# A recurrent mixer with two gated layers: each pair's inputs in three transfers, first key-value products earlier, first output sums later

## Chip, cores, metric

The kernel runs on one core of a Trainium2 chip. The metric is device microseconds of one execution, the median of several runs. Beside them there is one execution taken by the hardware profiler; every time of the trace below is counted in microseconds from the first instruction of that execution.

## What is computed

The reference, cut to what matters (batch 4, 8 heads, 768 steps, head size 48; 3072 tokens of width 384; hidden sizes 1536 and 2048):

```python
state = zeros(B, H, D, D)
for t in range(768):
    cur = einsum('bhd,bhe->bhde', u * k[t], v[t])
    y[t] = einsum('bhd,bhde->bhe', r[t], state + cur)
    state = w[t][..., None] * state + einsum('bhd,bhe->bhde', k[t], v[t])
x = y as (3072, 384)
x = (sigmoid(x @ w_gate) * (x @ w_val)) @ moe_w_out
h = x @ moe2_w_in
out = (h * tanh(softplus(h))) @ moe2_w_out
```

## The kernel before

**Tiling.** The 768 steps are cut into 24 steps j of 32 time steps; two of them are a pair p = 0..11. A pair gives 256 rows of the first gated layer, so the first layer runs as twelve rounds, one for each pair; two rounds give 512 rows of the second layer. Products are made of a high and a low half of type f16, so each weight exists twice (w_gate as wgs, w_val as wvs, moe_w_out as wos, moe2_w_in as wis, moe2_w_out as wps); the weights are decoded on the chip from 64-bit words (raw_wg, raw_wv, raw_wo, raw_wi, raw_wp) by ACT, DVE and POOL.

**A pair's own work ("attention").** `load_pair` (line 414) brings r, k and w of a pair into one tile blk, double buffered by the pair's parity: 1280 KB, of which r is 384, k 512 and w 384 KB. `fine` (457) makes on POOL products of r and k (tiles pt; 128x768 with u, then 128x384) and lets DVE sum them into A; between its three levels POOL multiplies r, k and w by w (blk<-blk). r and k are needed from the first product on, w from the first multiplication by w. `coarse` (548) flips r, k, w on DVE (RD, KD, WD), makes lp on PE, flips A into X and merges lp into it (line 618). `keys` (639) finishes k and flips it into KT, the last read of blk. `step` (664) makes for each j the output rows yp (`rows_out`, from X, v, RD and the state s), splits them into two halves xs (`split`, line 200) and brings them to xt, for the first two pairs by flips on PE (xp, line 699), later by a transposing DMA; it makes the next state from the key-value products kp (`outer`, 778, with the bank of PSUM that `next_at` names, three in turn) and loads v of step j+3.

**Rounds.** `gate(p, f)` (814) makes for one f of 12 the gate and value sums gv (18 matmuls, four banks pg in turn, three in round 0) and from them gt, on ACT and DVE. `out1(p, c, part)` (880) sums a quarter of the output o of column block c, in one bank, po; after the fourth quarter ACT and DVE split it into xo, and SP stores xo to x2d. Round p holds the gates of pair p, the output sums of pair p-1 and the attention of pair p+1. From 634 us on there is only the second layer: h (line 1013) and its output sums (1058).

**Order.** Nothing runs in the order of the code. `Plan.run` (87) plays all tasks with written costs, gives each a latest due time, and at each moment takes on each engine the ready task that is due first; the order that comes out is each engine's program. Who must wait for whom on the chip is then set by the tiles: a DMA into blk waits for the last reader of the pair two before. All DMAs of the page stand in the one queue of SP in the planned order, except the transposing ones, which ACT issues; an issue that waits holds all behind it. Every engine runs its own list in order.

The part of `load_pair` that sets how many transfers a pair has:

```python
if p:
    attn("sp", 3.6, lambda e: go(e, None), [], keys, lat=2.0)
else:
    attn("none", 0, new, [], keys, lat=0.0)
    for i in range(3):
        attn("sp", 1.2, lambda e, i=i: go(e, i), [], [keys[i]], lat=2.0)
```

Of the kernel before, what the change touches and what calls it, by code (L numbers as in the profile page):

```python
# [24 lines left out]
DM = H * D  # L25
# [126 lines left out]
def mixer_moe_kernel(  # L152
# [245 lines left out]
    kd = {}  # L398
    wd = {}
    lps = {}  # L400
    yps = {}
    kps = {}
    xss = {}
# [10 lines left out]
    def load_pair(p):  # L414
        edges = (0, C * DH, C * (DH + DP), BLK)

        def new(e):
            blk[p] = fp.tile([128, BLK], F32, tag=f"blk{p % 2}", name=f"blk{p}")

        def go(e, i):  # L420
            if i is None:
                new(e)
            cs = slice(0, BLK) if i is None else slice(edges[i], edges[i + 1])
            nc.sync.dma_start(out=blk[p][:, cs], in_=rkw[p, :, cs])

        keys = [("blk", p % 2, i) for i in range(3)]
        if p:
            attn("sp", 3.6, lambda e: go(e, None), [], keys, lat=2.0)
        else:
            attn("none", 0, new, [], keys, lat=0.0)  # L430
            for i in range(3):
                attn("sp", 1.2, lambda e, i=i: go(e, i), [], [keys[i]], lat=2.0)

    def load_v(j):
        def go(e):
# [228 lines left out]
    def step(j):  # L664
        p, e = divmod(j, 2)
        V = ("v", j % 3)
        S, nxt = ([("s", i % 2, x) for x in range(2)] for i in (j, j + 1))
        ybank = next_at()

        def rows_out(part):  # L670
            if not part:
# [43 lines left out]
                    out=xt[p][:, i, :, 128 * e : 128 * e + 128], in_=xss[j][:, i]  # L715
                )

        for part in range(2):
            attn(
                "pe",  # L720
                0.8 * (COLD if j < 4 else 1.0),
                lambda _, part=part: rows_out(part),
                [("X", p % 2), ("RD", p % 2), V, *S],
                [ybank],
                burst=True,
            )
        xs = ("xs", j % 2)
        split(
            xs,
            lambda: yps[j][:, :DM],  # L730
            lambda: xss[j][:, 0],
            lambda: xss[j][:, 1],
            SX,
            0.45,
            [ybank, "attention"],
            new_xs,
        )
        reads = [(*xs, 0), (*xs, 1)]
        room = [("xt", p % 2, 0, 0)] * e
        if p < 2:  # L740

            tbank = next_at()
            attn("pe", 0.6, flip_x, [*reads, "eye"], [tbank])
            attn("act", 0.48, lambda on: put(on, 0), [tbank, *room], [("xt", p % 2, e, 0)])
            room = [("xt", p % 2, 0, 0)]
            attn("dve", 0.48, lambda on: put(on, 1), [tbank, *room], [("xt", p % 2, e, 1)])
        else:
            new = [("xt", p % 2, e, i) for i in range(2)]
            attn("act", 0.15, send, [*reads, *room], new, lat=2.8)
        if j + 1 == NJ:  # L750
            return

# [14 lines left out]
        for hf in range(2):  # L767
            if j:
                attn(
                    {"pool": 1.05, "dve": 0.6},  # L770
                    0,
                    lambda on, hf=hf: decay(on, hf),
                    [S[hf], ("WD", p % 2)],
                    [nxt[hf]],
                )
            kbank = next_at()

            def outer(_, hf=hf, kbank=kbank):
                kps[j, hf] = pp.tile([128, 8, D], F32, tag=f"at{kbank[1]}", name=f"kp{j}_{hf}")
                for i in range(8):  # L780
                    x = 8 * hf + i
                    for o in (0, 32, 64, 96):
                        nc.tensor.matmul(  # L783
                            kps[j, hf][o : o + 32, i, :],
                            KT[o : o + 32, p % 2, HG * e + x, :],
                            vs[j][o : o + 32, x, :],
                            start=True,
                            stop=True,
                        )

            def join(_, hf=hf):
                s = ss[j + 1][:, 8 * hf : 8 * hf + 8]
                if j:
                    nc.vector.tensor_tensor(out=s, in0=kps[j, hf], in1=s, op=ALU.add)
                else:
                    nc.vector.tensor_copy(out=s, in_=kps[j, hf])

            cold = COLD if j < 4 else 1.0
            attn("pe", 0.8 * cold, outer, [("KT", p % 2), V], [kbank], burst=True)
            attn("dve", 0.55, join, [kbank], [nxt[hf]])  # L800
        if j + 3 < NJ:
            load_v(j + 3)

# [376 lines left out]
    for p in range(NP):  # L1180
        for f in range(NF1):
            if p + 1 < NP:
                if f == YPOS[0]:
                    tail1(p + 1)
                if f == YPOS[1]:
                    tail2(p + 1)
                    if p + 2 < NP:
                        cells[p + 2] = fine(p + 2)
                    else:
                        tail_end()  # L1190
            if f == 0 and p >= NP - 1:
                load_x2(0)
                load_x2(1)
            gate(p, f)
            if p > 0:
                out1(p - 1, f // 4, f % 4)
    add("none", 0, lambda e: None, [], ["gates", "free_g"])
    add(
        "act",
# [61 lines left out]
```

## Time and profile before

| | us |
|---|---|
| median of 3 runs (lowest to highest) | 1024.71 (1020.68 to 1025.45) |
| the profiled execution, its own time | 1025.36 |
| its span, first to last instruction | 1023.6 |
| PE busy in the span | 941.2 (92%) |
| DVE, ACT, POOL busy | 512.9, 347.1, 307.6 |
| mean granted clock of PE, of full speed | 0.988 |

The profile's page gives busy time by engine and, in 40 slices of 25.6 us, how busy each engine and the 16 DMA engines were. PE is idle for 82.4 us of the span, all of it in the first 634 us. A wait is put down to what ended it; "issue" stands for an idle time that ended with nothing that the profile shows. PEq, SPq and ACTq are the sequencers that hand instructions to an engine or a queue. The queue kind "instruction" in the DMA views carries programs to the engines.

### The profile page before, as it was taken

Reading aid. Unit: us, or ns where it says so; the run is one execution under the profiler, and the core shown is the slowest. Engines: PE = TensorE matmul, PEld = TensorE weight load, DVE = VectorE, ACT = ScalarE, POOL = GpSimd, SP = SyncE. Lnnn points to the kernel's source line nnn. Section 1 sums busy time; section 2 is a strip of 40 time slices with the busy share of each in tenths; the row PEclk is TensorE's granted clock in tenths of the full one; section 3 lists DMA queues with packets and bytes.
Section 4 is the critical chain, followed back from the end, with each engine's and each line's share of the span. In section 5 each row is a group of like instructions: output and inputs, shape, how many; then the busy total and the mean of one; then the engine's idle time right before and its main releaser. Section 6 shows DMA issues by size and latency. Waiting matters only on the chain.

```text
span 1023.6 us, 32777 instructions
## 1 busy us (share of the span) xinstructions
PE 941.2 (92%) x14952; PEld 678.8 (66%) x14952; DVE 512.9 (50%) x831; ACT 347.1 (34%) x693; POOL 307.6 (30%) x322
## 2 busy tenths in 40 slices
PE   0388789989999899989999999999999999999998
PEld 0266678868878687878888887655555555555555
DVE  5899988866666556666658557221111111111110
ACT  3347622212212122222226356433333333333320
POOL 8873589671744444454113011000000000000000
PEclk9999899989999899999999999999999999999999
DMA  9345543222140404040206351010100101000000
GB/s 303 125 168 177 198 95 110 45 100 91 33 91 29 90 28 90 29 100 20 60 9 173 107 175 42 11 37 16 41 14 16 39 16 47 9 16 16 8 16 31
DMA packets 53595, 72.12 MB, mean 70 GB/s; under 512 B 20432, under 2 KB 37328, under 8 KB 52048
## 3 DMA queue, kind: packets, MB, share of 16 engines
q1 hardware_dynamic: 36816, 66.09, 21.2%
q10 hardware_dynamic: 16640, 3.94, 2.4%
q8 instruction: 117, 1.92, 0.8%
q14 instruction: 22, 0.18, 0.1%
HBM read 56.64 MB, written 9.44 MB: 65 GB/s over the span
## 4 chain that ended last, share of the span: by engine, by line
PE 78%; DVE 9%; DMA 4%; issue 3%; POOL 2%; ACT 2%; ACTq 0%; SPq 0%; DVEq 0%
PE gv L828 22%; PE o L1058 18%; PE h L1013 18%; PE o L892 11%; PE yp L680 3%; PE kp L783 3%; PE lp L595 3%; DMA raw_wo<-wo 1%; POOL pt L455 1%; DVE A L476 1%; POOL blk L455 1%; DVE word_wi L286 1%; DMA raw_wp<-wo 1%; DMA raw_wv<-wv 1%; DVE X L611 1%
## 5 line engine op out<-in xcount | busy, mean ns | idle before, releaser
L1013 PE MATMUL h<-x,wis 128*128 128x512 f16 x864 | 201.5, 379 | 0.0
L828 PE MATMUL gv<-xt,wgs 128*128 128x256 f16 x1296 | 167.4, 277 | 11.7 <-DVE gt L859 5.7
L828 PE MATMUL gv<-xt,wvs 128*128 128x256 f16 x1296 | 168.1, 276 | 4.3 <-issue 4.3
L892 PE MATMUL o<-gt,wos 128*128 128x256 f16 x1296 | 167.5, 275 | 4.4 <-DVE xo L207 1.9
L455 POOL TENSOR_TENSOR blk<-blk 128x384 f32<-128x384 f32 (+1 forms) x144 | 125.9, 890 | 70.0 <-DVE KD L566 59.3
L828 PEld LDWEIGHTS <-wgs 128*128 128x128 f16 x1296 | 124.9, 99 | 30.5 <-issue 12.6
L1013 PEld LDWEIGHTS <-wis 128*128 128x128 f16 x864 | 84.5, 98 | 90.7
L892 PEld LDWEIGHTS <-wos 128*128 128x128 f16 x1296 | 127.2, 98 | 24.2 <-issue 4.8
L828 PEld LDWEIGHTS <-wvs 128*128 128x128 f16 x1296 | 121.9, 99 | 23.4 <-issue 4.6
L839 ACT ACTIVATE sig<-gv 128x256 f32<-128x256 f32 x144 | 55.0, 383 | 236.4 <-PE gv L828 225.2
L1024 ACT ACTIVATE e<-h 128x512 f32<-128x512 f32 x96 | 57.3, 597 | 207.5 <-PE h L1013 207.5
L455 POOL TENSOR_TENSOR pt<-blk 128x384 f32<-128x384 f32 (+1 forms) x96 | 108.4, 1154 | 51.4 <-DMA blk<-rkw 47.3
L844 DVE SCALAR_TENSOR_TENSOR gv<-gv,sig 128x256 f32<-128x256 f32 x144 | 61.7, 429 | 82.7 <-ACT sig L839 82.2
L856 ACT CAST gt<-gv 128x256 f16<-128x256 f32 x144 | 53.2, 371 | 76.1 <-DVE gv L844 69.1
L859 DVE TENSOR_TENSOR gt<-gv,gt 128x256 f16<-128x256 f32 x144 | 60.3, 419 | 32.2 <-ACT gt L856 32.1
L595 PE MATMUL lp<-RD,KD 64*16 64x16 f32 (+1 forms) x3072 | 34.5, 185 | 37.0 <-DVE RD L560 33.6
L1031 DVE SCALAR_TENSOR_TENSOR wos<-e,wos 128x512 f16<-128x512 f32 x27 | 18.7, 692 | 84.5 <-ACT wos L1027 84.5
L595 PEld LDWEIGHTS lp<-RD,KD 64*16 64x16 f32 (+1 forms) x3072 | 29.8, 101 | 46.1 <-DVE RD L560 33.6
L1058 PE MATMUL o<-wps,wgs 128*128 128x384 f16 x324 | 58.5, 326 | 0.0
L1058 PE MATMUL o<-wps,wos 128*128 128x384 f16 x324 | 57.2, 326 | 0.0
L1031 DVE SCALAR_TENSOR_TENSOR wgs<-e,wgs 128x512 f16<-128x512 f32 x27 | 18.7, 692 | 73.8 <-ACT wgs L1027 73.8
L783 PE MATMUL kp<-v,KT 32*32 32x48 f32 x2944 | 45.9, 212 | 8.6 <-issue 7.5
(92 smaller groups left out, 1051.0 us busy)
## 6 DMA issues: line engine op xcount, KB each, us to landing
blk<-rkw SPq DMA_DIRECT2D x11, 1280.0 KB, 6.7
v<-vt SPq DMA_DIRECT2D x96, 96.0 KB, 3.3
raw_wi<-wi SPq DMA_DIRECT2D x8, 768.0 KB, 4.9
raw_wp<-wo SPq DMA_DIRECT2D x8, 768.0 KB, 4.4
raw_wg<-wg SPq DMA_DIRECT2D x6, 768.0 KB, 4.5
raw_wv<-wv SPq DMA_DIRECT2D x6, 768.0 KB, 4.8
raw_wo<-wo SPq DMA_DIRECT2D x6, 768.0 KB, 4.4
x2d<-xo SPq DMA_DIRECT2D x36, 128.0 KB, 1.8
```

The costliest lines, as they stand in the source:

```text
L455: engines[e].tensor_tensor(out=pv, in0=a, in1=b, op=ALU.mult)
L595: nc.tensor.matmul(out, kd[p][gs, x, :m], rhs, start=True, stop=True, skip_group_check=True)
L783: nc.tensor.matmul(kps[j, hf][o : o + 32, i, :], KT[o : o + 32, p % 2, HG * e + x, :], vs[j][o : o + 32, x, :], start=True, stop=True,)
L828: nc.tensor.matmul(gps[p, f][:, o], w[:, a, kc, fs], xt[p][:, c, kc, :], start=(n == 0), stop=(n == 3 * KC - 1),)
L839: nc.scalar.activation(out=sgs[p, f], in_=gps[p, f][:, 0], func=AF.Sigmoid, scale=1.0 / (SW * SX))
L844: nc.vector.scalar_tensor_tensor(out=gps[p, f][:, 1], in0=gps[p, f][:, 1], scalar=SG / (SW * SX), in1=sgs.pop((p, f)), op0=ALU.mult, op1=A ...
L856: nc.scalar.copy(out=gt[p][:, 0, f], in_=gps[p, f][:, 1])
L859: nc.vector.tensor_tensor(out=gt[p][:, 1, f], in0=gps[p, f][:, 1], in1=gt[p][:, 0, f], op=ALU.subtract,)
L892: nc.tensor.matmul(ops[p, c][:, :NT], wos[:, a, f, cs], gt[p][:, g, f, :], start=(f == 0 and n == 0), stop=(f == NF1 - 1 and n == 2),)
L1013: nc.tensor.matmul(hps[r, f], w2["wi"][:, a, kc, fs], x2[r][:, c, kc, :], start=(n == 0), stop=(n == 3 * KC - 1),)
L1024: nc.scalar.activation(out=es[r, f], in_=hps[r, f], func=AF.Mish, scale=ih)
L1058: nc.tensor.matmul(ops2[r, t][:, :DM], g2[r][f][:, c, tsl], w2["wp"][:, a, f, :], start=(f == 0 and n == 0), stop=(f == NF2 - 1 and n == 2),)
```

## The change

Three edits, all in the task list that the plan works on.

1. Pairs 0, 2 and 3 are loaded in three transfers (r, k, w) that are queued one after the other. Pairs 4 to 11 have them apart: r is listed where the whole load was (round p-3, gate 7), k after gate 11 of round p-3 and after the last store of out1 of that round, w after gate 3 of round p-2 and after the first store of that round. Pair 1 keeps one transfer.
2. In step 0 the key-value products and the state made of them are listed ahead of the outputs, and take their banks first.
3. The twelve quarters of out1 of pair 0 are listed two at a time behind gates 6 to 11 of round 1, not one behind each gate.

```diff
+    late = {}
@@ load_pair
-        if p:
+        if p == 1:
             attn("sp", 3.6, lambda e: go(e, None), [], keys, lat=2.0)
-        else:
-            attn("none", 0, new, [], keys, lat=0.0)
-            for i in range(3):
-                attn("sp", 1.2, lambda e, i=i: go(e, i), [], [keys[i]], lat=2.0)
+            return
+
+        after = [[], [("x2d", p - 4, KC - 1)], [("x2d", p - 3, 0)]]
+        attn("none", 0, new, [], keys, lat=0.0)
+        for i in range(3):
+            late[p, i] = lambda i=i: attn(
+                "sp", 1.2, lambda e: go(e, i), after[i] if p > 3 else [], [keys[i]], lat=2.0
+            )
+            if p <= 3 or i == 0:
+                late.pop((p, i))()
@@ step
-        ybank = next_at()
+        ybank = tbank = None
...
+        def outputs():
+            nonlocal ybank, tbank
+            ybank = next_at()
...
+        if j:
+            outputs()
         if j + 1 == NJ:
             return
...
             attn("dve", 0.55, join, [kbank], [nxt[hf]])
+        if not j:
+            outputs()
@@ the loop over rounds p and gates f
             gate(p, f)
-            if p > 0:
+            if p > 1:
                 out1(p - 1, f // 4, f % 4)
+            elif p == 1 and f >= 6:
+                for n in (2 * f - 12, 2 * f - 11):
+                    out1(0, n // 4, n % 4)
+            if f == 3 and p > 1 and (p + 2, 2) in late:
+                late.pop((p + 2, 2))()
+            if f == 11 and (p + 3, 1) in late:
+                late.pop((p + 3, 1))()
```

The body of `outputs` is what stood in `step` before, moved in by one level.

**The queue of SP around the turn from round 5 to round 6** (blk7 to blk10 are pairs, v a step's values, x2d<-xo a store of the first layer's output). Before:

```order
L928 DMA x2d_86<-xo_5408 128x512
L424 DMA blk9_5815<-rkw 128x2560
L440 DMA v15_5915<-vt 32x768 x4
L928 DMA x2d_86<-xo_5788 128x512
L440 DMA v16_6118<-vt 32x768 x4
L928 DMA x2d_86<-xo_6148 128x512
```

Changed:

```order
L945 DMA x2d_86<-xo_5753 128x512
L447 DMA v15_5834<-vt 32x768 x4
L447 DMA v16_6082<-vt 32x768 x4
L425 DMA blk9_6099<-rkw 128x768
L945 DMA x2d_86<-xo_6112 128x512
L425 DMA blk8_5214<-rkw 128x1024
L945 DMA x2d_86<-xo_6245 128x512
L425 DMA blk8_5214<-rkw 128x768
```

The whole load of pair 9 ahead of v15 has become r of pair 9 behind v16; k and w of pair 8 stand behind the stores of o14_2 and o15_0, a round later than its whole load stood before.

**DVE at the same turn** (gv6_0 is the first gate of round 6, pt the product with u that POOL makes of r and k, A its sums, xo<-o15_0 what the second of those stores sends). Before:

```order
L455 TENSOR_TENSOR pt_5943<-pt_5943,U_93 128x768
L844 SCALAR_TENSOR_TENSOR gv5_11_6059<-gv5_11_6059,sig_6135 128x256
L207 SCALAR_TENSOR_TENSOR xo_6148<-o14_2_5866,xo_6148 128x256
L476 TENSOR_REDUCE A_91<-pt_5943 128x32
L859 TENSOR_TENSOR gt5_5321<-gv5_11_6059,gt5_5321 128x256
```

Changed:

```order
L876 TENSOR_TENSOR gt6_6153<-gv6_1_6117,gt6_6153 128x256
L462 TENSOR_TENSOR pt_6198<-pt_6198,U_93 128x768
L861 SCALAR_TENSOR_TENSOR gv6_2_6178<-gv6_2_6178,sig_6222 128x256
L483 TENSOR_REDUCE A_91<-pt_6198 128x32
L207 SCALAR_TENSOR_TENSOR xo_6245<-o15_0_6139,xo_6245 128x256
```

The product with u, which waits for POOL and so for k, has moved from the end of round 5 to behind gate 1 of round 6, three instructions ahead of the split of o15_0.

**PE at the start, from the first lp on** (kp0_0 and kp0_1 are the two halves of the first key-value products; the flips xp0 follow in both). Before:

```order
L595 MATMUL lp0_242<-RD0_232,KD0_229 32x24 x64
L595 MATMUL lp0_242<-RD0_232,KD0_229 16x16 x64
L680 MATMUL yp0_398<-v0_114,X0_226 32x48 x16
L783 MATMUL kp0_0_419<-v0_114,KT_92 32x48 x32
L680 MATMUL yp0_398<-v0_114,X0_226 32x48 x16
L699 LDWEIGHTS xs0_484
```

Changed:

```order
L602 MATMUL lp0_242<-RD0_232,KD0_229 32x24 x64
L602 MATMUL lp0_242<-RD0_232,KD0_229 16x16 x64
L798 MATMUL kp0_0_395<-v0_114,KT_92 32x48 x32
L798 MATMUL kp0_1_434<-v0_114,KT_92 32x48 x32
L688 MATMUL yp0_475<-v0_114,X0_226 32x48 x16
L688 MATMUL yp1_497<-v1_124,X0_226 32x48 x4
```

Both halves of kp0 stand ahead of yp0; kp0_1 stood behind the six flips xp0 before, and yp1, which needs the state made of both, behind that.

**DVE at the end of round 0's gates** (word_wo is the decoding of moe_w_out). Before:

```order
L286 SCALAR_TENSOR_TENSOR word_wo4_1734<-raw_wo4_1569,word_wo4_1734 128x768
L275 SCALAR_TENSOR_TENSOR word_wo5_1783<-word_wo5_1783,low_wo5_1771 128x768
L300 TENSOR_TENSOR wos_90<-word_wo4_1734,wos_90 128x768
L286 SCALAR_TENSOR_TENSOR word_wo5_1783<-raw_wo5_1707,word_wo5_1783 128x768
L859 TENSOR_TENSOR gt0_807<-gv0_11_1686,gt0_807 128x256
```

Changed:

```order
L876 TENSOR_TENSOR gt0_778<-gv0_11_1579,gt0_778 128x256
L612 TENSOR_TENSOR KD2_1208<-KD2_1208,WD2_1600 128x32x8
L612 TENSOR_TENSOR RD2_1424<-RD2_1424,WD2_1600 128x32x8
L275 SCALAR_TENSOR_TENSOR word_wo0_1468<-word_wo0_1468,low_wo0_1526 128x768
L618 STREAM_TRANSPOSE X2_1830<-A_91 128x32x32
```

All decoding of moe_w_out, which stood ahead of the last gate of round 0, now begins behind it.

## Rows read from the trace of the kernel before

**Rows 1.** The page's span, busy times and PE's line of its 40 slices.

```profile
span 1023.6 us, 32777 instructions
PE 941.2 (92%) x14952; PEld 678.8 (66%) x14952; DVE 512.9 (50%) x831; ACT 347.1 (34%) x693; POOL 307.6 (30%) x322
...
PE   0388789989999899989999999999999999999998
...
```

**Rows 2.** PE's waits from 190 to 460 us: total, times, longest.

```profile
PE gv L828 <- issue: 8.6, 2, 4.3
PE yp L680 <- issue: 3.8, 2, 2.7
PE o L892 <- issue: 1.8, 1, 1.8
PE kp L783 <- issue: 0.8, 2, 0.4
```

**Rows 3.** The same view from 460 to 634 us, where no pair is loaded.

```profile
PE gv L828 <- DVE gt L859: 1.3, 1, 1.3
PE o L892 <- DVE xo L207: 1.0, 3, 0.5
```

**Rows 4.** Stretches: length, PE, PEld, DVE, ACT, POOL busy (instructions), PEclk, DMA share, GB/s.

```profile
160.00:170.00 10.00, 10.00 (x94) 8.96 (x92) 9.25 (x15) 3.92 (x9) 9.84 (x9) 1.00 0.42 144
...
200.00:210.00 10.00, 5.66 (x163) 4.47 (x162) 4.78 (x7) 1.52 (x4) 0.42 (x1) 0.94 0.93 228
208.80:215.60 6.80, 5.83 (x85) 4.18 (x86) 1.37 (x4) 0.76 (x2) 5.87 (x6) 0.50 0.24 63
352.10:358.90 6.80, 5.59 (x84) 3.94 (x84) 0.95 (x1) 0.00 (x0) 4.20 (x5) 0.50 0.11 19
...
500.00:510.00 10.00, 10.00 (x206) 8.65 (x204) 6.61 (x12) 2.18 (x6) 0.83 (x1) 1.00 0.28 75
```

**Rows 5.** DMA queues from 341.5 to 350.5 us: packets, MB, share.

```profile
q1 hardware_dynamic: 298, 1.64, 80.6%
q10 hardware_dynamic: 832, 0.20, 20.3%
```

**Rows 6.** The same view from 500 to 512 us, the program's own queue.

```profile
q8 instruction: 2, 0.03, 1.2%
```

**Rows 7.** PE in order of time: start, length, instructions, [idle before, what ended it].

```profile
47.31 0.36 PE L783 MATMUL kp<-v,KT 32*32 32x48 f32 x2 [3.73 <-issue]
...
411.84 2.13 PE L828 MATMUL gv<-xt,wgs 128*128 128x256 f16 x18
...
421.67 1.15 PE L892 MATMUL o<-gt,wos 128*128 128x256 f16 x9
...
425.39 0.82 PE L892 MATMUL o<-gt,wos 128*128 128x256 f16 x6
```

**Rows 8.** SP's issues around the turn from one round to the next.

```profile
393.67 0.33 SPq L424 DMA_DIRECT2D blk<-rkw  x1
...
412.91 0.34 SPq L928 DMA_DIRECT2D x2d<-xo  x1
```

**Rows 9.** POOL after that load.

```profile
399.88 2.75 POOL L455 TENSOR_TENSOR pt<-blk 128x768 f32<-128x768 f32 x2 [5.99 <-DMA blk<-rkw]
402.71 1.98 POOL L455 TENSOR_TENSOR blk<-blk 128x384 f32<-128x384 f32 x2
```

**Rows 10.** The loads of blk: a piece of pair 0 (count, KB, us to landing); all loads.

```profile
blk<-rkw SPq DMA_DIRECT2D x2, 384.0 KB, 4.1
...
DMA to landing us min/median/max: 3.2/6.3/10.5
```

**Rows 11.** PE's waits from 61 to 180 us.

```profile
PE gv L828 <- DVE gt L859: 4.5, 3, 2.4
...
PE lp L595 <- POOL KD L605: 2.0, 1, 2.0
```

**Rows 12.** Decoding moe_w_out on DVE: count, ns min/median/max, first and last start.

```profile
L275 DVE SCALAR_TENSOR_TENSOR word_wo<-word_wo,low_wo x6: 926/951/1379, 95.5 to 119.6; 128x768 uint32<-128x768 uint32 x6
```

More of the change, by code (lines that the diff above doesn't have):

```diff
@@ L716, in send @@
                 )
[L718 to L725, printed above, removed]
-            )
[L727 to L749, printed above, removed]
+        def outputs():
+            nonlocal ybank, tbank
+            ybank = next_at()
+            for part in range(2):
+                attn(
+                    "pe",
+                    0.8 * (COLD if j < 4 else 1.0),
+                    lambda _, part=part: rows_out(part),
+                    [("X", p % 2), ("RD", p % 2), V, *S],
+                    [ybank],
+                    burst=True,
+                )
+            xs = ("xs", j % 2)
+            split(
+                xs,
+                lambda: yps[j][:, :DM],
+                lambda: xss[j][:, 0],
+                lambda: xss[j][:, 1],
+                SX,
+                0.45,
+                [ybank, "attention"],
+                new_xs,
+            )
+            reads = [(*xs, 0), (*xs, 1)]
+            room = [("xt", p % 2, 0, 0)] * e
+            if p < 2:
+                tbank = next_at()
+                attn("pe", 0.6, flip_x, [*reads, "eye"], [tbank])
+                attn("act", 0.48, lambda on: put(on, 0), [tbank, *room], [("xt", p % 2, e, 0)])
+                room = [("xt", p % 2, 0, 0)]
+                attn("dve", 0.48, lambda on: put(on, 1), [tbank, *room], [("xt", p % 2, e, 1)])
+            else:
+                new = [("xt", p % 2, e, i) for i in range(2)]
+                attn("act", 0.15, send, [*reads, *room], new, lat=2.8)
```

## The prediction

> **What bounds the kernel now.** I read the page first, to see which engine has no room: PE is busy for 941 of 1023.6 us and full from the 25th slice on, so whatever is gained must come out of the first 634 us, where its slices hold 7s and 8s [rows 1]. I then asked for PE's waits by stretch, since an average over the start, the rounds and the second layer says nothing on any of them. From 190 to 460 us PE waited in seven places, 15.0 us together, and every one ended with "issue": it waited for no engine [rows 2]. From 460 to 634 us, with the same rounds but no pair left to load, not one such wait is listed and 2.3 us are lost in all [rows 3]. So the difference between the two stretches is the thing to explain.
>
> What is special about the seven places shows in the stretches and the queues. From 200 to 210 us the 16 DMA engines were 0.93 busy while PE was busy for 5.66 of 10 us; from 500 to 510, with loads of v and transposing DMAs but no pair, 0.28 and 10.00 [rows 4]. In the 9 us around the load of 340.9 us only the two data queues moved packets; of the queue that carries PE's program there is none, while in 12 undisturbed us it moves two [rows 5, 6]. My reading: PE runs out of program because the blocks of its program arrive behind 1280 KB of a pair. One row supports that from the other side: at 160 to 170 us a pair is loaded too (DMA 0.42) and PE does not stop, because there it issues only 94 matmuls in 10 us, against 163 in the 5.7 busy us of the stretch at 200 [rows 4]. A load hurts where yp and kp run, with hundreds of short matmuls, and not where gates run.
>
> The longest two waits cost more than their length: at 208.8 to 215.6 and 352.1 to 358.9 us the granted clock was 0.50, the lower level of 1.2 GHz, just after PE had stood idle for over 4 us [rows 2, 4]. PE was busy there for 5.83 and 5.59 us, half of which, 5.7 us, is lost. The load of pairs therefore costs 15.0 + 5.7 = 20.7 us now.
>
> The Trainium skill says otherwise of the mechanism: Runtime: NRT & Kernel Launch, Instruction fetch mechanics, has the program streamed in 16 KiB blocks ahead of need, with the cost of crossing a block "mostly hidden". By that page the seven waits would not be the load's doing, and the sum would be the start-up term alone; the rows at 200 and 341.5 us speak against it, and it stands below as a rival.
>
> **Edit 1, three transfers apart.** It removes nine loads of 1280 KB and adds 27 smaller ones. On SP that is 18 issues more of 0.33 us each, on a queue that waits most of the time: nothing on PE's path. What matters is where the pieces fall. Let T0 be the first gate of a round, 411.84 in the example [rows 7]. The last store of the round before was issued at T0 + 1.1 [rows 8]; r now stands ahead of it, behind v, and k right behind it, so k is issued at about T0 + 1.5. That is the stretch of pure gates in which a load did no harm. w stands behind the store of the first output sum, whose last quarter ends at T0 + 10.8; the split and the store bring w to about T0 + 12.7, alone, with 384 KB. The dense matmuls at the end of a round keep only v and the transposing DMAs, as from 460 us on. So nearly the whole 20.7 should go. What I hold back is the turn into round 2 and round 2 itself, where k and w of pair 4 share the queue with raw_wi3 and raw_wi4, 768 KB each: 3.2 us. I take **17.5 us**; ends 12 and 20.7.
>
> Edit 1 also adds waits. Behind k: POOL's product for u, and behind that DVE's product with u, after which gate 2, a sum and the split of the first output block stand on DVE. The next output sum on PE needs that split, since there is one bank, and it begins at T0 + 13.5 [rows 7]. Counting back four operations of DVE (split, sum, gate, product) at no more than the 0.95 us of a 128x768 one [rows 12] and one of POOL at 1.4 (half of the first of [rows 9]), k must have landed by about T0 + 8.3. How long it takes is not in the trace: a piece of 384 KB took 4.1 us, the whole pair from issue to POOL's start 6.2 us [rows 8 to 10], which gives T0 + 5.6 to 7.7. v, r and k together are 1280 KB, so I take the later, and 0.6 us of room. w: with 4.1 us it lands at T0 + 16.8, and POOL needs two multiplications by w (1.98 us [rows 9]), four products and three more by w, some 9 us at a us each, before DVE asks for the third sum, at about T0 + 26.5 by PE's list at 1 us for nine matmuls. That leaves about 0.7 us. I price both waits at nothing, with that cover; without it each us late costs PE a us in each of seven rounds.
>
> **Edits 2 and 3, the start.** kp0 now stands whole ahead of yp0 and of the flips xp0, so the next state and yp1 can come sooner; but PE stood still for 3.73 us inside kp0_0, by issue, during two large loads [rows 7], and those loads are still there, in four pieces. The gates of round 0 run beside the decoding on DVE and wait for it (gv for gt, 4.5 us [rows 11]): a gate that starts sooner would only wait longer. What makes room there is edit 3: twelve operations of decoding moe_w_out, the first six at a median 0.95 us [rows 12], some 12 us, leave the list ahead of round 0's last gate and come back in round 1, where PE has enough other work. The waits that they can have caused are at most 6.5 us (4.5 + 2.0 [rows 11]). Against it: raw_wg4 now stands behind the three pieces of pair 3 on SP, which wait for KT of pair 1, and the output sums of pair 0 wait for POOL, which has all six low halves of wos to make between products for pair 3. The upper bound is 3.7 + 6.5 = 10.2 us; the lower one is a loss, which I bound by a second wait like the one for KD, 2 us [rows 11], since raw_wg4 feeds gates that PE can put off in favour of attention. Most of what DVE puts off comes back before round 2, so I take **3 us**, near the lower end of the gain.
>
> The second layer, from 634 us on, keeps its order and its 389 us. Decoding moe2_w_in begins later, but has room until 634 us: nothing.
>
> **Sum.** 17.5 + 3 = 20.5 us of the profiled execution's 1025.4 gives 1004.9; the median of the runs lies 0.65 below that execution, so **1004**. Its own ends: 20.7 + 10.2 off gives 994, 12 less a loss of 2 gives 1015.
>
> **Rivals.**
> *The pieces still crowd.* v, r, the store and k fall within 4 us at the turn, 1408 KB, where the load and v made 1664. If the block that PE needs is still late there, half of the 20.7 stays; with nothing or a small gain at the start, 6 to 10 us are gained: 1015 to 1019. For it: r and v still go out together, and k follows them by no more than some 3 us. Against it: the row at 160 us [rows 4]. Chance 0.14.
> *The waits are not the load's doing.* Then only the start's 3 us come: 1021.7, no difference that can be told. Rows 2 and 3 side by side speak against it. By the page on instruction fetch this would be the forecast; the trace does not bear it out. Chance 0.09.
> *k and w arrive too late (slower).* POOL starts late, DVE stands in order behind it, and PE waits for the one output bank, in seven rounds. The longest landing of a load was 10.5 us [rows 10]; k at that is at T0 + 12.0, 3.7 over, and w at T0 + 23.2, some 5.7 over. Not every landing will be the longest, so I take half of the two together, 4.7 us a round: 7 x 4.7 = 33 us are lost against 20.5 gained, 1037. It decides from (20.5 + 5) / 7 = 3.6 us a round on. For it: the room is only 0.6 and 0.7 us. Against it: the long landings belong to loads in a crowd of 2 MB. Chance 0.11.
>
> **Chances and range.** The forecast has 0.66. About 0.5%, 5 us, is what a measurement of this kernel can tell from no change. Faster by more: the forecast and the first rival, 0.8; no difference 0.09; slower 0.11. The range reaches from the forecast's lower end over the first rival, 994 to 1019.
>
> **What would show it.** Right: no issue waits over 1 us between 190 and 460 us, no stretch there at the 0.50 clock, rounds equally long before and after the last load, the program's queue with a packet in every 5 us of dense matmuls; k landed by T0 + 8.3, so no wait of output sums for DVE's split beyond the 1.0 us of [rows 3]. At the start: the first gate 2 to 5 us sooner and fewer waits of gv for gt. Wrong: "PE o <- DVE xo" or "DVE pt <- POOL pt" growing with every round (the slower rival), issue waits that move to the turn (the crowd), or long waits for POOL's wos in round 1 (edit 3).

## The result, and the profile after

| | before | changed |
|---|---|---|
| median of 4 runs each (lowest to highest), us | 1022.69 (1018.63 to 1025.45) | 1009.27 (1008.22 to 1010.89) |
| ratio to before (95% interval) | | 0.987 (0.984 to 0.991) |
| profiled execution, its span, us | 1025.36, 1023.6 | 1009.48, 1007.8 |
| PE busy in the span, us | 941.2 | 934.3 |
| issue waits of PE from 190 to 460 us | 15.0 | none |
| mean granted clock of PE in the profiled execution, of full speed | 0.988 | 0.985 |

The changed kernel is faster by some 13 us (1.3%). The forecast was 1004, with a range of 994 to 1019: the time lies inside, 5 us above the point. The direction and its cause held; the gain was forecast too large.

The page of the changed kernel, its busy times and PE's 40 slices, to be laid beside [rows 1]: from the 7th slice to the last but one every slice of PE is full, where the kernel before still had 8s at the 9th, the 14th and the 18th; the slices of the start, 7s and a 6, are less full than before (8s and a 7).

```profile
PE 934.3 (93%) x14952; PEld 677.2 (67%) x14952; DVE 520.0 (52%) x830; ACT 345.9 (34%) x691; POOL 314.4 (31%) x325
...
PE   0377679999999999999999999999999999999998
```

**The rounds** are counted from 0, as the pairs are. The list of PE's waits from 190 to 460 us, which held the seven waits of [rows 2], is empty for the changed kernel. One stretch of it answers to the stretch at 200 us of [rows 4] (columns as there): the same dense matmuls of yp and kp, more of them, beside loads of v and the transposing DMAs, with PE full and the clock at 1.00.

```profile
380.00:390.00 10.00, 10.00 (x316) 8.48 (x316) 8.71 (x11) 2.65 (x7) 4.97 (x6) 1.00 0.42 75
```

The first sigmoid of each round is a good mark. Of the changed kernel's rounds the lengths between these marks are 45.7 us, five times in a row from round 5 to round 10, the same to within 0.01 us; before, the same five went from 45.7 to 52.8. From the mark of round 2 to that of round 11 it took 419.0 us, before 436.5. The last round before that mark, with no pair left to load, is longer in the changed kernel, 48.5 us (before 44.1), with two waits of 1.6 and 1.8 us for DVE in it; the prediction had named equal rounds as a sign.

These lengths hold unlike amounts of work. Here are PE's matmuls of the first layer's output sums up to the mark of round 2 and from there to that of round 11 (stretch, length, PE busy and count, PEld busy and count, PEclk, DMA share, GB/s). Before:

```profile
0.00:166.24 166.24, 16.22 (x117) 11.43 (x117) 0.97 0.56 175
166.24:602.74 436.50, 125.03 (x974) 95.75 (x975) 0.98 0.27 70
```

Changed:

```profile
0.00:167.07 167.07, 11.94 (x84) 8.36 (x85) 0.91 0.53 160
167.07:586.09 419.02, 128.09 (x1008) 98.22 (x1005) 1.00 0.28 76
```

Edit 3 has put 33 matmuls of output sums past the mark of round 2. Of the gates' matmuls there are 453 and then 1953 before, 450 and 1946 in the changed kernel. So the changed kernel does 27 matmuls more between the two marks and 36 fewer ahead of them. At 0.98 us for nine, as gates and sums follow each other here, that is an estimated 2.9 and 3.9 us. On equal work the rounds gained some 20.4 us, not 17.5.

**The turn of a round**, of which the prediction asked whether k and w come in time. First SP's issues around the turn from round 6 to round 7, the turn of the prediction's example; the first gate of round 7 starts at T0 = 397.25 us. Then what POOL, DVE and PE do with k and w.

```profile
398.42 0.35 SPq L425 DMA_DIRECT2D blk<-rkw  x1
398.87 0.37 SPq L945 DMA_DIRECT2D x2d<-xo  x1
399.29 0.42 SPq L425 DMA_DIRECT2D blk<-rkw  x1
409.12 0.33 SPq L945 DMA_DIRECT2D x2d<-xo  x1
409.50 0.43 SPq L425 DMA_DIRECT2D blk<-rkw  x1
```

```profile
403.62 2.76 POOL L462 TENSOR_TENSOR pt<-blk 128x768 f32<-128x768 f32 x2 [4.54 <-DMA blk<-rkw]
...
414.06 1.97 POOL L462 TENSOR_TENSOR blk<-blk 128x384 f32<-128x384 f32 x2 [0.48 <-DMA blk<-rkw]
```

```profile
408.67 0.42 DVE L207 SCALAR_TENSOR_TENSOR xo<-o,xo 128x256 f16<-128x256 f32 x1 [0.28 <-ACT xo L204]
```

```profile
410.80 1.15 PE L909 MATMUL o<-gt,wos 128*128 128x256 f16 x9
```

The three blk issues are r, k and w. k goes out at T0 + 2.0, POOL starts on it at T0 + 6.4; the split of the output block ends at 409.09, 1.7 us before PE asks for the bank, at T0 + 13.5. w goes out at T0 + 12.3 and POOL has it at T0 + 16.8.

**The start** did not get shorter. The first gate comes 2.3 us sooner (its mark stands at 63.9 us, before at 66.2), but the mark of round 2 stands at 167.1 us, before at 166.2, with 36 matmuls fewer done: on equal work that is a loss of some 4.8 us. These are PE's waits up to 190 us; [rows 11] shows some of the same lines of before.

```profile
PE lp L602 <- DVE RD L567: 36.2, 1, 36.2
PE yp L688 <- DVE X L625: 6.1, 1, 6.1
PE gv L845 <- DVE gt L876: 3.7, 3, 1.8
...
PE yp L688 <- issue: 3.1, 2, 1.7
PE o L909 <- POOL wos L300: 2.8, 2, 1.9
...
PE kp L798 <- DVE KT L661: 1.8, 1, 1.8
PE kp L798 <- issue: 1.5, 2, 1.2
PE lp L602 <- issue: 1.2, 2, 0.6
```

From the mark of round 11 to the end it takes 421.7 us, before 420.9; eight matmuls of gates more (198 against 190) stand behind that mark, which is all of the 0.8 us. PE's waits from 460 to 634 us, 2.3 us in [rows 3], sum to 4.1.

### The profile page after: what moved, and what is told of

It reads as the page before. It is cut to its first block, busy times and chain, and to the rows that moved or that the text cites. A ratio compares the mean times of both kernels' runs of the same rounds, so it can differ in the third digit from the quotient of the medians.

```text
span 1007.8 us, 32811 instructions
## 1 busy us (share of the span) xinstructions
PE 934.3 (93%) x14952; PEld 677.2 (67%) x14952; DVE 520.0 (52%) x830; ACT 345.9 (34%) x691; POOL 314.4 (31%) x325
## 4 chain that ended last, share of the span: by engine, by line
PE 79%; DVE 9%; DMA 4%; POOL 3%; ACT 2%; issue 1%; ACTq 1%; SPq 0%; DVEq 0%
PE gv L845 22%; PE o L1075 19%; PE h L1030 19%; PE o L909 12%; PE yp L688 3%; PE kp L798 3%; PE lp L602 2%; DMA raw_wg<-wg 2%; POOL pt L462 1%; POOL blk L462 1%; DVE word_wi L275 1%; POOL wos L300 1%; DMA raw_wv<-wv 1%; ACTq L722 1%; DMA raw_wp<-wo 1%
## 5 line engine op out<-in xcount | busy, mean ns | idle before, releaser
L845 PE MATMUL gv<-xt,wgs 128*128 128x256 f16 x1296 | 165.1, 275 | 3.9 <-DVE gt L876 3.7
L462 POOL TENSOR_TENSOR blk<-blk 128x384 f32<-128x384 f32 (+1 forms) x144 | 128.3, 903 | 69.6 <-DVE WD L580 51.0
L602 PE MATMUL lp<-RD,KD 64*16 64x16 f32 (+1 forms) x3072 | 34.7, 184 | 40.7 <-DVE RD L567 36.2
L602 PEld LDWEIGHTS lp<-RD,KD 64*16 64x16 f32 (+1 forms) x3072 | 29.9, 101 | 49.9 <-DVE RD L567 36.2
L483 DVE TENSOR_REDUCE A<-pt 128x32 f32<-128x768 f32 (+1 forms) x60 | 51.5, 862 | 0.5 <-POOL pt L462 0.5
```

What stands on the lines that cost most here:

```text
L462: engines[e].tensor_tensor(out=pv, in0=a, in1=b, op=ALU.mult)
L483: nc.vector.tensor_reduce(out=cell(), in_=shape(pts.pop(n)), op=ALU.add, axis=AX.X)
L602: nc.tensor.matmul(out, kd[p][gs, x, :m], rhs, start=True, stop=True, skip_group_check=True)
L845: nc.tensor.matmul(gps[p, f][:, o], w[:, a, kc, fs], xt[p][:, c, kc, :], start=(n == 0), stop=(n == 3 * KC - 1),)
```

## The experiments

Theory: the whole gain is the load's. While 1280 KB of a pair come in beside the dense matmuls of yp and kp, blocks of PE's program arrive late; taken apart in time, they don't. Rivals: the gain is that of the other order (edits 2 and 3); the size of a single transfer counts, not its place; the waits were made by the order or by the readers of a whole load, and not by bytes.

| kernel | us | ratio to before (95%) | issue waits 0 to 190, 190 to 460 us |
|---|---|---|---|
| changed kernel, twice | 1009.3, 1007.5 | 0.987 (0.984 to 0.991), 0.987 (0.984 to 0.991) | 5.8, 0; 8.0, 0 |
| edit 1 alone, twice | 1006.7, 1008.3 | 0.986 (0.983 to 0.989), 0.986 (0.983 to 0.990) | 9.5, 0; 9.2, 0 |
| edits 2 and 3 | 1023.8 | 1.002 (1.000 to 1.004) | 10.0, 11.3 |
| three transfers at the old place | 1021.1 | 1.000 (0.997 to 1.002) | 5.9, 13.1 |
| one transfer at the turn | 1016.4 | 0.994 (0.992 to 0.996) | 7.3, 0 |
| copies, early | 1013.7 | 0.992 (0.990 to 0.995) | 19.6, 0 |
| copies of 1280 KB at the old place | 1024.9 | 1.002 (1.000 to 1.005) | 6.9, 9.8 |
| copies of 640 KB there | 1012.6 | 0.990 (0.987 to 0.994) | 6.8, 2.9 |
| edits 1 and 2 | 1010.6 | 0.989 (0.986 to 0.992) | 6.1, 0 |
| edits 1 and 3 | 1008.2 | 0.988 (0.985 to 0.991) | 15.3, 0 |
| edit 1, pairs 2 and 3 later | 1007.9 | 0.986 (0.983 to 0.989) | 3.2, 0 |

The runs of the experiments came in three groups, each with its own runs of the kernel before (medians 1021.1, 1022.9 and 1023.5); so the ratios are compared, not the times.

### Edit 1 alone

The diff is edit 1 of the change; `step` and the listing of the output sums stay as they were.

```diff
             gate(p, f)
             if p > 0:
                 out1(p - 1, f // 4, f % 4)
+            if f == 3 and p > 1 and (p + 2, 2) in late:
+                late.pop((p + 2, 2))()
+            if f == 11 and (p + 3, 1) in late:
+                late.pop((p + 3, 1))()
```

> Only the spreading of the pairs' loads (edit 1); the first key-value products and the first output sums stand as before. Theory (the whole gain is the load's, taken from the rounds behind 190 us): no issue wait over 1 us from 190 to 460 us, 1005 to 1011 us, ratio to before 0.983 to 0.989. Rival (the order at the start, edits 2 and 3, carries part of the gain): half of it is missing, 1015 to 1019 us.

1006.7 us, 0.986 (0.983 to 0.989): the theory's number, and as large a gain as the whole change's. From 190 to 460 us no wait is listed, as in the changed kernel. From the mark of round 2 to that of round 11 it takes 414.2 us, 22.3 less than before; it has nine matmuls of gates and sums fewer there, so that some 21.3 us are gained on equal work.

### Edits 2 and 3 without the first

```diff
-        if p == 1:
+        if p:
             attn("sp", 3.6, lambda e: go(e, None), [], keys, lat=2.0)
...
-            if f == 3 and p > 1 and (p + 2, 2) in late:
-                late.pop((p + 2, 2))()
-            if f == 11 and (p + 3, 1) in late:
-                late.pop((p + 3, 1))()
```

> Only edits 2 and 3; every pair from 1 on comes in one transfer at its old place. Theory (the load's): the seven issue waits between 190 and 460 us and the half-clock stretches after them are all there, 13 to 17 us of waits; only the start differs, 1019 to 1026 us. Rival (the order at the start carries part): 1013 to 1017 us.

1023.8 us, 1.002 (1.000 to 1.004): no gain, if anything a loss. PE's waits from 190 to 460 us have the four lines of [rows 2] again, 11.3 us by issue where before had 15.0 and the theory 13 to 17, and two half-clock stretches, 6.8 us together where before had 13.7:

```profile
PE gv L839 <- issue: 5.3, 2, 2.8
PE yp L682 <- issue: 2.7, 2, 1.6
PE kp L792 <- issue: 2.0, 3, 1.1
PE o L903 <- issue: 1.3, 1, 1.3
```

So the gain is edit 1's; the order rival falls.

### Three transfers, all at the old place

```diff
         for i in range(3):
-            late[p, i] = lambda i=i: attn(
-                "sp", 1.2, lambda e: go(e, i), after[i] if p > 3 else [], [keys[i]], lat=2.0
-            )
-            if p <= 3 or i == 0:
-                late.pop((p, i))()
+            attn("sp", 1.2, lambda e, i=i: go(e, i), [], [keys[i]], lat=2.0)
```

> As the changed kernel, but r, k and w of a pair are listed together where its whole load was listed, so that the same 1280 KB come in three transfers close to one another, in the dense matmuls of yp and kp. Theory (it is the bytes in that stretch that hold the program's blocks up): issue waits of 8 to 15 us from 190 to 460 us, 1016 to 1025 us. Rival (it is the size of one transfer): a block slips in between two transfers, waits under 3 us, 1007 to 1012 us.

1021.1 us, 1.000 (0.997 to 1.002). Cut into three but not taken apart, the load costs all that it cost before; that it is three transfers counts for nothing here. The waits from 190 to 460 us, and the stretch with the longest:

```profile
PE kp L793 <- issue: 4.7, 3, 2.9
PE gv L840 <- issue: 4.0, 1, 4.0
PE yp L683 <- issue: 3.7, 2, 2.7
...
PE o L904 <- issue: 0.7, 1, 0.7
```

```profile
350.00:360.00 10.00, 5.98 (x148) 4.40 (x146) 4.51 (x5) 0.86 (x2) 6.37 (x6) 0.71 0.55 122
```

The clock of 0.71 in it is a mean: from 354.2 to 361.1 us it was at the lower level of 1.2 GHz, from 1.4 us before the end of a wait of 4 us on, as with the two waits of 4.3 us in the kernel before [rows 2, 4].

This kernel shows best how such a wait ends. The DMA queues (packets, MB, share of 16 engines) from 343 to 352.8 us, then in the 0.2 us behind, then PE's first matmul after the wait:

```profile
q1 hardware_dynamic: 613, 1.45, 79.0%
q10 hardware_dynamic: 832, 0.20, 16.7%
```

```profile
...
q8 instruction: 1, 0.02, 43.1%
```

```profile
355.60 1.23 PE L840 MATMUL gv<-xt,wgs 128*128 128x256 f16 x5 [4.02 <-issue]
```

For 9.8 us no packet of PE's program starts; one does between 352.8 and 353.0, it takes 1.4 us, and 1.4 us after its end PE goes on. It is the same at every issue wait over 0.3 us from 190 to 460 us in the traces of the kernel before and of the four kernels here that have such waits (edits 2 and 3, this one, and the two with copies at the old place): PE goes on 1.2 to 1.7 us after a packet of that queue has ended, but for one wait of 0.7 us in this kernel, with 3.0. In the changed kernel, from 379 to 397 us, such packets start 3.9 to 5.0 us apart. That is what [rows 5, 6] only suggested.

### One transfer at the turn

```diff
+        late[p, 0] = lambda: attn(
+            "sp", 3.6, lambda e: go(e, None), [("x2d", p - 4, KC - 1)], keys, lat=2.0
+        )
...
-            if f == 3 and p > 1 and (p + 2, 2) in late:
-                late.pop((p + 2, 2))()
-            if f == 11 and (p + 3, 1) in late:
-                late.pop((p + 3, 1))()
+            if f == 11 and (p + 3, 0) in late:
+                late.pop((p + 3, 0))()
```

> As the changed kernel, but from pair 4 on a pair comes in one transfer of 1280 KB, listed where k is in the changed kernel: at the turn of the round, behind the last store, among pure gates. Theory (it is the place): no issue wait over 1 us from 190 to 460 us, 1007 to 1012 us, as the changed kernel. Rival (it is the size of one transfer): issue waits of 8 us or more, now in the gates, 1016 to 1025 us. POOL has the pair later than before; if r comes too late for its first product, waits of DVE for POOL show it, 1 to 3 us a round.

1016.4 us, 0.994 (0.992 to 0.996): both were half wrong. No issue wait is left from 190 to 460 us, so a load of 1280 KB does no harm to PE's program among gates, and the size of one transfer is not what matters. But 7 us of the gain are lost otherwise. First a stretch with the load in it, then what PE and POOL wait for from 190 to 460 us:

```profile
400.00:410.00 10.00, 10.00 (x105) 8.79 (x105) 3.76 (x7) 2.65 (x7) 4.21 (x4) 1.00 0.42 144
```

```profile
PE gv L846 <- DMA xt<-xs: 3.8, 5, 1.3
```

```profile
POOL pt L463 <- DMA blk<-rkw: 78.0, 6, 18.1
```

PE now waits at the turn of the round for the last transposing DMAs. In the changed kernel POOL waits 30.5 us in that stretch for blk, here 78.0, since r comes with the rest. All attention work begins later and ends after PE has run out of gates. I read the chain from these lines; no run here moved r alone. From the mark of round 5 to that of round 11 this kernel takes 285.0 us, the changed one 277.2; 13 of its matmuls of gates and sums fewer stand behind that mark, so some 6.4 of the 7.8 us are lost. If the reading is right, that is what it is worth here to have r ahead of the rest.

### Copies that nobody reads

The third rival is left: that the order, or the readers of a whole load, made the waits. So I added transfers that nothing reads: rows of a pair, copied from memory to another place in memory.

```diff
+    def extra(p):
+        def go(e):
+            t = dram.tile([128, 2560], F32, tag="extra", name=f"extra{p}")
+            nc.sync.dma_start(out=t, in_=rkw[p, :, :2560])
+
+        attn("sp", 3.6, go, [], ["extra"], lat=2.0)
...
             load_pair(p + 2)
+            if p + 2 > 3:
+                extra(p + 2)
```

> The changed kernel with one more transfer of 1280 KB for each pair from 4 on: the pair's rows are copied to a place in memory that nothing reads, queued where the whole load stood before, in the dense matmuls of yp and kp. Nothing waits for it but what is queued behind. Theory (bytes in that stretch hold up PE's program): issue waits are back, 8 to 16 us from 190 to 460 us, all between the end of one round's gates 7 and its last, 1019 to 1030 us. Rival (the waits came from the order of the instructions in the kernel before, or from the readers of a whole load): none over 1 us, 1007 to 1012 us.

1013.7 us, 0.992 (0.990 to 0.995), with no issue wait from 190 to 460 us. The theory's time was missed, and for a fault of mine: a copy without a condition is ready at once, so the plan put all eight of them into the first 62 us, and not where the loads stood. So this run does not test what it was made for. PE's issue waits up to 190 us, 8.0 us in the changed kernel that ran beside it, are 19.6:

```profile
PE yp L695 <- issue: 6.1, 3, 3.2
PE kp L805 <- issue: 5.8, 4, 2.8
PE lp L609 <- issue: 4.6, 1, 4.6
PE gv L852 <- issue: 3.1, 2, 2.8
```

That fits the theory, but up to 190 us the kernels without copies differ too, from 3.2 to 15.3 us in the table, so this run shows little. In the next kernel each copy waits, in the plan, for the store of the second output block of its round, so that it is queued just ahead of the loads of v, where the whole load of a pair had been, in rounds 2 to 8.

```diff
-            t = dram.tile([128, 2560], F32, tag="extra", name=f"extra{p}")
-            nc.sync.dma_start(out=t, in_=rkw[p, :, :2560])
+            t = dram.tile([128, BLK + 8], F32, tag="extra", name=f"extra{p}")
+            nc.sync.dma_start(out=t[:, :BLK], in_=rkw[p])
...
-        attn("sp", 3.6, go, [], ["extra"], lat=2.0)
+        attn("sp", 3.6, go, [("x2d", p - 4, 1)], ["extra"], lat=2.0)
...
-            if p + 2 > 3:
-                extra(p + 2)
...
+            if f == 7 and p > 1 and p + 3 < NP:
+                extra(p + 3)
```

> The changed kernel with one more transfer of 1280 KB in each of rounds 2 to 8: a pair's rows are copied to a place in memory that nothing reads. Other than in the first run of this kind, each copy is queued behind the store of the second output block of its round, just ahead of the two loads of v, which is where the whole load of a pair stood before. Theory (bytes in the dense matmuls hold up PE's program): issue waits of 8 to 16 us from 190 to 460 us, 1018 to 1028 us. Rival (the waits were the order's or the readers'): none over 1 us, 1007 to 1012 us.

1024.9 us, 1.002 (1.000 to 1.005): seven copies that nothing reads take back the whole gain. All of PE's waits from 190 to 460 us, and the copies (count, KB each, median us to landing):

```profile
PE yp L695 <- issue: 4.8, 3, 2.3
PE gv L852 <- issue: 2.0, 1, 2.0
PE kp L805 <- issue: 1.9, 3, 1.1
PE o L916 <- issue: 1.1, 1, 1.1
```

```profile
extra<-rkw SPq DMA_DIRECT2D x7, 1280.0 KB, 8.0
```

From the mark of round 2 to that of round 11 this took 434.5 us, against 419.0 in the changed kernel: 15.5 us more, of which the waits by issue up to 640 us are 11.4 and one half-clock stretch of 3.4 us some 1.7. Some 2 us I can't place; the list of waits leaves out the very short ones. The expectation's time of 1018 to 1028 holds. The rival falls: in this trace and in the next ACT, DVE and POOL run the same operations in the same order as in the changed kernel, SP issues the same transfers but for the copies, and PE's order differs only in runs of yp, of which a trace can lack some records. No wait for a transfer stands in PE's list, so v, which is queued behind a copy, is not what PE waited for.

The last of them halves the dose, `rkw[p, :, : BLK // 2]`, at the same place:

> As the run before it, with 640 KB instead of 1280 in each copy. Theory (bytes, with room for about a transfer like those of v or of a third of a pair before PE runs out): some waits, a quarter or less of those with 1280 KB, 0 to 4 us, 1008 to 1013 us. Rival (proportional to the bytes): half of them, 4 to 8 us, 1013 to 1019 us.

1012.6 us, 0.990 (0.987 to 0.994). The waits by issue from 190 to 460 us:

```profile
PE gv L852 <- issue: 1.3, 1, 1.3
PE kp L805 <- issue: 1.1, 1, 1.1
PE yp L695 <- issue: 0.5, 1, 0.5
```

2.9 us against 9.8: three tenths of the waits for half of the bytes. It lies inside the theory's 0 to 4 us, a little over its quarter, and under the rival's 4 to 8. In these two executions the waits grew faster than the bytes; each is one execution, and the whole loads alone cost 11.3 to 15.0 us in three, so the form of the growth is not shown.

### The start: edits 2 and 3, one at a time

The changed kernel beside itself, as a control for the two kernels that follow:

> The changed kernel once more, beside the kernels that follow, so that parts of it are compared on one chip. Both theories: 1008 to 1011 us.

It took 1007.5 us. Edit 1 with edit 2 (the output sums of pair 0 are listed behind every gate of round 1, as before):

```diff
-            if p > 1:
+            if p > 0:
                 out1(p - 1, f // 4, f % 4)
-            elif p == 1 and f >= 6:
-                for n in (2 * f - 12, 2 * f - 11):
-                    out1(0, n // 4, n % 4)
```

> Edits 1 and 2: spread loads and the first key-value products ahead of the outputs; the output sums of pair 0 stand one behind each gate of round 1 as before. Theory (edit 3 costs the 2 to 3 us by which the changed kernel lies behind edit 1 alone, since PE waits for POOL's wos and has less to do at the start of round 1): 1005 to 1008 us. Rival (edit 2 costs it): 1009 to 1012 us.

1010.6 us, 0.989 (0.986 to 0.992): the rival's number. Edit 1 with edit 3 (`step` as before):

```diff
-        if j:
-            outputs()
...
-        if not j:
-            outputs()
```

> Edits 1 and 3: spread loads and the output sums of pair 0 in the second half of round 1; the first step as before. Theory (edit 3 costs 2 to 3 us): 1008 to 1011 us. Rival (edit 2 costs it): 1005 to 1008 us.

1008.2 us, 0.988 (0.985 to 0.991), in the range of the theory and at the edge of the rival's. The two runs contradict each other as to which edit costs, and all intervals here overlap: the medians alone don't rank these kernels. The traces say a little more. By the mark of round 5, up to which all of them have done the same number of matmuls (before took 313.9 us) and from which on each of them goes on at the same pace, the start took 306.0 and 305.8 us with edit 1 alone, 306.1 with edits 1 and 3, 308.9 and 306.8 with all three, 310.4 with edits 1 and 2. The waits of gates for DVE up to 190 us, with edits 1 and 2 and then with edits 1 and 3:

```profile
PE gv L845 <- DVE gt L876: 9.8, 5, 4.2
```

```profile
PE gv L835 <- DVE gt L866: 1.7, 2, 1.4
```

With edit 1 alone it is 4.0 and 2.8, with all three 3.7 and 4.4. So edit 3 seems to give DVE the room that I had expected of it, and edit 2 to take it away again; that rests on one or two executions of each. In time, the two together come to a loss of 1 to 3 us in these executions.

Since 9.5 us of issue waits up to 190 us were left with edit 1 alone, I also tried to take pairs 2 and 3 apart further. I had it run with edit 1 once more:

> Edit 1 alone once more, beside a variant of its start. Both theories: 1005 to 1009 us.

That took 1008.3 us. In the variant k and w of pair 2 go behind gates 1 and 3 of round 0, those of pair 3 behind gate 11 of round 0 and gate 3 of round 1:

```diff
+    early = {(3, 1): [("gt", 0, 11, 1)], (3, 2): [("gt", 1, 3, 1)], (2, 1): [("gt", 0, 1, 1)], (2, 2): [("gt", 0, 3, 1)]}
...
-                "sp", 1.2, lambda e: go(e, i), after[i] if p > 3 else [], [keys[i]], lat=2.0
+                "sp", 1.2, lambda e: go(e, i), after[i] if p > 3 else early.get((p, i), []), [keys[i]], lat=2.0
...
-            if p <= 3 or i == 0:
+            if p < 2 or i == 0:
...
-            if f == 3 and p > 1 and (p + 2, 2) in late:
+            if p == 0 and f in (1, 3):
+                late.pop((2, 1 + f // 3))()
+            if f == 3 and p > 0 and (p + 2, 2) in late:
```

> Edit 1 alone, with k and w of pairs 2 and 3 put later too: k and w of pair 2 behind the second and the fourth gate of round 0, k of pair 3 behind the last gate of round 0, w behind the fourth gate of round 1. With edit 1 alone PE waits 9.5 us by issue before 130 us. Theory A (these are the pairs' bytes again, beside the weights'): half of these waits or more go and the start is 3 to 6 us shorter, 1001 to 1004 us. Rival B (up to there DVE, with its decoding, sets the pace): the waits by issue go and waits for DVE come in their place, 1005 to 1010 us.

1007.9 us, 0.986 (0.983 to 0.989), no better than edit 1 alone. Issue waits up to 190 us fell from 9.5 to 3.2; in their place stand waits for DVE and POOL:

```profile
PE gv L836 <- DVE gt L867: 6.2, 5, 2.1
...
PE o L900 <- POOL wos L300: 3.5, 3, 1.4
```

Rival B's time and waits came: all of PE's waits up to 190 us are 62.1 us here, 61.8 with edit 1 alone, so a wait by issue that goes is replaced by another. No kernel here beats edit 1 alone by more than can be measured, and it can't be told from the changed kernel either.

## Why the prediction held, and where its size was off

**What bounds the kernel: right.** The seven waits that end with "issue" were the load's doing. Taking the loads apart removed them, edits 2 and 3 did not, and copies without a reader brought them back. The step from [rows 2, 3] to [rows 4 to 6], that one stretch with loads and one without differ by just these waits, carried the prediction. A slip beside it changed no term: the edit removes ten loads of 1280 KB and adds 30 smaller ones, 20 issues more and not 18.

**The price of the waits, 20.7 us: right for the execution that it was taken from; the base was too high.** Between the marks the rounds gained 17.5 us, the very number taken, but by luck: 2.9 us of matmuls had moved in among them. On equal work they gained some 20.4, and some 21.3 with edit 1 alone, so the 3.2 us held back for the turn into round 2 were not needed. But the waits differ from one execution to the next: 15.0 us in the profiled one of before, 11.3 and 13.1 in two kernels whose loads stand at the same place. Its 1025.36 us lie near the upper end of the four runs of before, at 1018.63 to 1025.45, and the runs beside the experiments had medians down to 1021.1. I took off the gain from a median of three runs, 1024.71, that was 1 to 4 us high. The first step that failed in size is "the median of the runs lies 0.65 below that execution": it treated a cost that varies as fixed. The second is the start's 3 us, below.

**The clock: right for the rounds, without a term for the start.** No half-clock stretch is left from 190 us on, where before had 13.7 us. But up to 190 us the changed kernel had 30.6 us of it, before 10.3. These are two of its stretches, 49.6 to 59.8 and 117.9 to 131.5 us:

```profile
49.60:59.80 10.20, 6.99 (x213) 5.59 (x202) 8.88 (x11) 3.51 (x7) 5.91 (x7) 0.50 0.48 141
117.90:131.50 13.60, 7.93 (x266) 6.95 (x267) 12.14 (x16) 5.56 (x10) 13.60 (x10) 0.50 0.50 155
```

The first comes 13 us after PE's first matmul, in a stretch of short waits; the second begins while yp waits 6.1 us for X (116.2 to 122.4 us). The prediction had no term for it. With edit 1 alone it is 17.2 and 13.6 us, with edits 1 and 2 37.4, and those two are the ends of the starts' lengths above too, 306 and 310.4 us. Over all traces, the kernels with edit 2 have 17.0 to 37.4 us of it up to 190 us, those without 10.3 to 23.9. The waits and the clock hang together, so I can't say how much of the start's loss is the clock's; no run separates them.

**Edits 2 and 3, +3 us: wrong.** By the mark of round 2 the trace had lost 0.9 us, some 4.8 on equal work (1.1 us sooner, so some 2.8 lost, in the second execution of the changed kernel). Edit 1 alone lost 2.6 and 2.2 us there with the same number of matmuls done as before, and edits 2 and 3 without the first made the whole kernel 0.2% slower (0 to 0.4). The first gate did come sooner, inside the 2 to 5 us of the forecast. What the sum left out is what comes later in place of the waits that went. kp0, put ahead of yp0, waits for KT (1.8 us); the output sums of pair 0 wait for POOL's wos (2.8), which the prediction had named as a danger and given no term of its own; the waits for X are no shorter (6.1 us, before 4.5). Issue waits at the start went only from 7.2 to 5.8 us, and to 8.0 in the second execution. Part of the loss is none of the change's: pair 1's load landed 8.9 us after its issue in this execution,

```profile
16.95 1.81 POOL L462 TENSOR_TENSOR pt<-blk 128x768 f32<-128x768 f32 x1 [3.06 <-DMA blk<-rkw]
```

so POOL began with it at 16.95 us, before at 15.29, with the same issues ahead of it; the first lp then came 2.6 us later (36.2 against 33.6). In the second execution of the changed kernel POOL began at 15.78 us, the first lp came after 34.7 and the mark of round 2 stood at 165.2.

**The second layer and the end: right.** Priced at nothing; the 0.8 us more behind the mark of round 11 are eight matmuls that moved there.

**The rivals.** *The pieces still crowd* fell: not one issue wait is left from 190 to 460 us. The case against it, that a load among gates is harmless, held even for 1280 KB at once. *The waits are not the load's doing* fell with the copies. The Trainium skill (Runtime: NRT & Kernel Launch, Instruction fetch mechanics) calls the cost of crossing a 16 KiB boundary of the program "mostly hidden". The trace agrees with it where gates run, and shows up to 4.3 us for one block that comes late beside a large load. *k and w arrive too late* fell for the pieces: k was used at T0 + 6.4, inside the 5.6 to 7.7 worked out, with 1.7 us left before PE asked for the bank, where 0.6 was forecast; w came at T0 + 16.8, as counted. With all three put off, in the kernel with one transfer at the turn, late pairs did cost time, some 7 us and not the 33 of the rival.

## What to carry to other kernels

A load that nobody waits for can still stop an engine, if it comes while that engine runs many short instructions: an idle time that ends with "issue" beside a busy DMA share, and a program queue with no packet in it, is the sign. Move the load to where long instructions run, and let the piece that is needed first go first (that last is read from one kernel's waits); cutting it up without moving it gave nothing. Before a gain is subtracted, see how the cost itself spreads over several executions, and don't count on a gain in a stretch that several engines fill (here the start) unless all of them get less to do. And where a change moves work past the mark that a stretch is measured by, count the work on each side of it.

## What was not expected of the hardware

- PE goes on 1.2 to 1.7 us after the end of a packet of its program's queue, at all but one of the issue waits over 0.3 us from 190 to 460 us in five traces. Beside a load of 1280 KB there were 7 to 10 us between the starts of two such packets ahead of the waits of over 2 us.
- Half of the bytes made three tenths of the waits (2.9 against 9.8 us, one execution each).
- The granted clock fell to its lower level before the end of each wait of 4.0 to 4.3 us in the rounds. Around the end of those of 2.5 to 2.9 us it fell with edits 2 and 3 (209.0 to 212.4 and 352.4 to 355.8 us) and not in the kernel before or with three transfers at the old place; and with copies of 1280 KB it fell behind one of 1.75 us (449.8 to 453.2 us), not behind one of 2.3. The length of the wait alone does not say it.
